# Key and value transfers of a whole batch (8 heads, 32 KB per partition), with the keys of a batch in two halves that have their own maxima

## The chip, the cores and the metric

The kernel runs on one core of a Trainium2 chip. The metric is the time of one execution in microseconds of the device. Three runs of the kernel before gave 190.66, 191.05 and 191.10 us; the median is 191.05.

The engines are named as in the profile: PE is the matmul engine (PEld its weight loads), DVE the vector engine, ACT the scalar engine, POOL GpSimd, and SP the engine that issues nearly all transfers here.

## The reference

One token of each of 8 batches passes through two branches, which a gate joins. All arrays are bfloat16. Branch A is attention over the last W = 1024 keys of a cache, with 16 query heads that share 8 key and value heads of 256 values each; branch B is a small MLP.

```python
g = sigmoid((x * gate_w).sum(-1, keepdims=True))           # x: (8, 1, 448)
q = (x @ wq).reshape(8, 1, 16, 256)                        # wq: (448, 4096)
k, v = k_cache[:, :, 3072:4096], v_cache[:, :, 3072:4096]  # (8, 8, 1024, 256), each head for 2 query heads
p = softmax(q k^T / 16)
a = (p v).reshape(8, 1, 4096) @ wo                         # wo: (4096, 448)
b = gelu(layernorm(x) @ w1 + b1) @ w2 + b2                 # hidden width 1792
out = g * a + (1 - g) * b
```

The window of keys and values is 8 batches x 8 heads x 1024 x 256 values, 33.55 MB of keys and as much of values, 67.1 MB of the 77.7 MB that the kernel reads.

## The kernel before

**Slots and loads.** Everything big goes through a ring of RING = 9 slots of 16 KB per partition (`ring`). `plan` is the list of loads in order; `pump` issues a load as soon as the program text has released enough slots with `done`, and the load itself then waits on SP until the slot's last readers are finished. SP issues in order, so a load that waits holds back the ones after it. The order is: keys of unit 0 in two parts, wq in two slots, w1, w2, then keys of unit u and values of unit u - 2 in turn, the last two values, and wo in two slots (the last piece cut in three, so that the end waits for little).

**Units.** A unit u (16 of them, NQ) is four key heads of one batch. `kv_loader` puts 4 heads x 1024 keys into a slot: partition p = 4 s + a holds 32 consecutive keys (NCK) of head a, segment s of 32. That is one row of 16 KB in memory for each partition, 2.1 MB in all.

**What a unit does.** `turn_keys` transposes half a slot in 32 x 32 blocks on DVE (line 357). `scores` puts the maskings of foreign heads (line 423) and eight matmuls (line 429) into half of a 1024-column PSUM tile S; two halves make a unit. `top` takes the maximum per partition (line 441), `share` joins the maxima of partitions by a matmul (449), `expo` makes the exponential with the row sums (455, 458). `turn` transposes the exponentials (471), `total` sums the row sums by a matmul (482), `invert` makes their reciprocals (492, 493), `values` multiplies with the values in 16 matmuls into PO (501) and takes the first half of it (510), `gather` adds the second half (516), and `finish` puts the normalized heads into oT (531, 534).

**The order of work.** It is written out by hand (`manual_schedule`): each engine carries its instructions out in the order of the program text. The loop at line 614 interleaves units: at u it turns and scores unit u, takes maxima and exponentials of unit u - 1, turns and multiplies unit u - 2 (LAG), and finishes unit u - 3. Before the loop come constants, `norm_and_gate`, the keys of unit 0, `query` (which makes qw, the query weights, from line 365 on), `mlp_hidden`, scores of unit 0 and `mlp_out` (line 592). After it come the rest of the last two units, `spread_rows` (656, 663), `project` (672), which multiplies with wo, and the final mix (690).

**Buffers that matter here.** Three transposed key tiles (`ktpool`), two S tiles, two small PSUM tiles shared by mz, den and fin (`ps_sm`), one PO, and one PSUM tile shared by hT, bb and A_ps (`ps_misc`).

Of the kernel before, what the change touches and what calls it, by code (L numbers as in the profile page):

```python
# [18 lines left out]
def kernel(  # L19
# [40 lines left out]
    RQ = QUAD * rep  # L60
    NQ = NB * Hkv // QUAD
    SK = P // QUAD
    NCK = W // SK
    NH = 2
    CH = NCK // NH
    NU = NQ
    SLOT = 8192
# [3 lines left out]
    WO_PARTS = [[(0, NJ8)]] * (NHQ - 1) + [[(0, 4), (4, 6), (6, 8)]]  # L71
    RING = 9
    LAG = 2
# [13 lines left out]
    ktpool = ctx.enter_context(tc.tile_pool(name="ktpool", bufs=3))  # L87
    epool = ctx.enter_context(tc.tile_pool(name="epool", bufs=2))
    opool = ctx.enter_context(tc.tile_pool(name="opool", bufs=LAG + 1))
# [19 lines left out]
    def kv_loader(src, u, parts):  # L109
        b, half = divmod(u, Hkv // QUAD)  # L110
        v = src[b, half * QUAD : (half + 1) * QUAD, kv_base:Sk, :].rearrange(
            "a (s c) d -> s a (c d)", c=NCK
        )

        def load(t):
            n = NCK * Dh // parts
            for i in range(parts):
                nc.sync.dma_start(  # L118
                    t[:, i * n : (i + 1) * n], v[:, :, i * n : (i + 1) * n]
                )  # L120

        return load
# [22 lines left out]
    def add_kv(name, src, u, parts=1):  # L145
        add((name, u), kv_loader(src, u, parts))
# [8 lines left out]
    add_kv("k", A_k_cache, 0, parts=2)  # L155
    add(("wq", 0), rows_loader([wq_m[:, 0 : 2 * HD]]))
    add(("wq", 1), rows_loader([wq_m[:, 2 * HD : 3 * HD], wq_t]))
    add(("w1",), rows_loader([w1_m, w1_t]))
    add(("w2",), rows_loader([w2_v]))
    for u in range(1, NQ):  # L160
        add_kv("k", A_k_cache, u)
        if u >= LAG:
            add_kv("v", A_v_cache, u - LAG)
    for u in range(NQ - LAG, NQ):
        add_kv("v", A_v_cache, u)
    for q in range(0, NHQ, 2):
        add(
            ("wo", q),
            rows_loader(
                [  # L170
                    wo_v[:, q + i, j0 * D : j1 * D]
                    for i in range(2)
                    for j0, j1 in WO_PARTS[q + i]
                ]
            ),
        )
# [4 lines left out]
    consts.tile([P, 448], BF16, name="pad")  # L181
# [37 lines left out]
    AREA = P + BLK  # L219
    qw = consts.tile([P, NJ, NU, AREA], BF16)  # L220
# [23 lines left out]
    for h in range(2):  # L244
# [18 lines left out]
    nc.vector.reduce_sum(sel2[:], pairs, axis=AXIS.X)  # L263
    nc.vector.reduce_sum(own[:], pairs.rearrange("p q i -> p i q"), axis=AXIS.X)
    head = consts.tile([BLK, QUAD], F32)
    nc.vector.reduce_sum(
        head[:],
        ident[0:BLK, 0:BLK].rearrange("p (s a) -> p a s", a=QUAD),
# [6 lines left out]
    for i in range(rep):  # L275
        nc.vector.tensor_copy(
            foreign[0:BLK, :].rearrange("p (b r) -> p b r", b=QUAD)[:, :, i:RQ:rep],
            head[:].rearrange("p (o a) -> p o a", o=1).to_broadcast([BLK, QUAD, QUAD]),
        )
# [73 lines left out]
    def turn_keys(u, hf):  # L353
        kn = slot("k", u)
        kt = ktpool.tile([P, CH, NK, BLK, NPAR], BF16, tag="kt", name="kt")
        KT[u, hf] = kt
        nc.vector.transpose(  # L357
            kt[:].rearrange("p c k x r -> p (c k x r)").bitcast(WORD),
            kn[:, hf * CH * Dh : (hf + 1) * CH * Dh].bitcast(WORD),
        )  # L360
        if hf == NH - 1:
            done()

    def query():
        for r in range(NR + 1):
            w, o = slot("wq", r // 2), (r % 2) * HD
            for n in range(W // QN):
                for t in range(QUAD):
                    col = t * W + n * QN
                    half, c = divmod(col, HH) if r == NR else (0, col)  # L370
                    nc.tensor.matmul(  # L371
                        Sq[32 * t : 32 * t + NB, n * QN : (n + 1) * QN],
                        lhsT=xT[:, r + half, :],
                        rhs=w[:, o + c : o + c + QN],
                        start=(r == 0),
                        stop=(r == NR),
                        skip_group_check=True,
                    )
        done(2)
# [15 lines left out]
        qp = ps_s.tile([P, NJ, NU, QUAD, RQ], F32, tag="S", name="qp")  # L395
        for j in range(NJ):
            for kk in range(NK // NJ):
                for par in range(NPAR):
                    nc.tensor.matmul(
                        qp[:, j, :, kk * NPAR + par, :],  # L400
                        lhsT=pick[:, kk, par, :],
                        rhs=qd[:, j].rearrange("p b h q i -> p (b h) (q i)"),
                        start=True,
                        stop=True,
                    )
        for b in range(QUAD):
            rows = slice(BLK * b, BLK * (b + 1))
            for j in range(NJ):
                dst = qw[rows, j, :, BLK * b : BLK * (b + 1)]
                src = qp[rows, j].rearrange("p u m q -> p u (m q)")  # L410
                if j == 0:
                    nc.scalar.copy(dst, src)  # L412
                else:
                    nc.vector.tensor_copy(dst, src)  # L414
# [3 lines left out]
    def scores(u, hf):  # L418
# [7 lines left out]
        for k in range(NK):  # L426
            for par in range(NPAR):
                j, m = k // (NK // NJ), k % (NK // NJ) * NPAR + par
                nc.tensor.matmul(  # L429
                    S[u][:, cols],  # L430
                    lhsT=qw[:, j, u, m * RQ : m * RQ + P],
# [19 lines left out]

    def expo(u):
        mz = soft.pop(u)
        nmx = epool.tile([P, 1], F32, tag="nmx", name="nmx")
        nc.vector.reduce_max(nmx[:], mz[:], axis=AXIS.X, negate=True)  # L455
        E = epool.tile([P, NCK // PAIR, BLK, PAIR], BF16, tag="E", name="E")
        rowsum = epool.tile([P, 1], F32, tag="rowsum", name="rowsum")
        nc.scalar.activation(  # L458
            E[:].rearrange("p c x i -> p c i x"),
            S.pop(u)[:].rearrange("p (c i x) -> p c i x", i=PAIR, x=BLK),  # L460
            ACT.Exp,
            bias=nmx[:],
            scale=1.0,
            accum_out=rowsum[:],
        )
        soft[u] = (E, rowsum)

    def turn(u):
        E, rowsum = soft.pop(u)
        ET = epool.tile([P, NCK // PAIR, BLK, PAIR], BF16, tag="ET", name="ET")  # L470
# [4 lines left out]
        soft[u] = (ET, rowsum)  # L475
# [3 lines left out]
    def total(u):  # L479
        ET, rowsum = soft.pop(u)  # L480
        den[u] = ps_sm.tile([P, 1], F32, tag="sm", name="den")
        nc.tensor.matmul(  # L482
            den[u][:], lhsT=rowden[:], rhs=rowsum[:], start=True, stop=True
        )
        soft[u] = ET

    rsel = {}

    def invert(u):
        rsel[u] = opool.tile([P, RQ], F32, tag="rsel", name="rsel")  # L490
        rb = epool.tile([P, 1], F32, tag="rb", name="rb")
        nc.vector.reciprocal(rb[:], den.pop(u)[:])  # L492
        nc.scalar.activation(rsel[u][:], sel2[:], ACT.Copy, scale=rb[:])  # L493

    def values(u):
        ET = soft.pop(u)
        vn = slot("v", u)
        NG = NCK // PAIR
        for c in range(NG):
            t = c % QUAD  # L500
            nc.tensor.matmul(  # L501
                PO[32 * t : 32 * t + PAIR * RQ],
                lhsT=ET[:, c, 0:RQ, :],
                rhs=vn[:, PAIR * c * Dh : PAIR * (c + 1) * Dh],
# [3 lines left out]
        done()  # L508
# [17 lines left out]
    def finish(u):  # L526
        b, half = divmod(u, Hkv // QUAD)
        os_, rs = soft.pop(u), rsel.pop(u)
        sm = ps_sm.tile([P, NJ, RQ], F32, tag="sm", name="fin")
        for j in range(NJ):  # L530
            nc.tensor.matmul(  # L531
                sm[:, j, :], lhsT=os_[:, j::NJ], rhs=rs[:], start=True, stop=True
            )
        nc.scalar.copy(  # L534
            oT[:, half * RQ : (half + 1) * RQ, :, b].rearrange("p h j -> p j h"), sm[:]
        )
# [70 lines left out]
    for hf in range(NH):  # L607
        turn_keys(0, hf)
    query()
    hs = mlp_hidden()  # L610
    for hf in range(NH):
        scores(0, hf)
    mlp_out(hs)
    for u in range(1, NQ):
        turn_keys(u, 0)
        scores(u, 0)
        if u >= LAG + 1:
            gather(u - LAG - 1)
        if u >= LAG:
            turn(u - LAG)  # L620
            total(u - LAG)
        if u >= LAG + 1:
            finish(u - LAG - 1)
        top(u - 1)
        share(u - 1)
        turn_keys(u, 1)
        if u >= LAG:
            values(u - LAG)
            invert(u - LAG)
        scores(u, 1)  # L630
        expo(u - 1)
    u = NQ - 1
    A_ps = ps_misc.tile([P, DO], F32, tag="misc", name="A_ps")
    gather(u - 2)
    finish(u - 2)
    turn(u - 1)
    total(u - 1)
    values(u - 1)
    top(u)
    share(u)  # L640
    invert(u - 1)
    expo(u)
    gather(u - 1)
    finish(u - 1)
    turn(u)
    total(u)
    invert(u)
# [19 lines left out]
    def project(q):  # L667
        w = slot("wo", q - q % 2)
        for j in range(NJ8):
            o = ((q % 2) * NJ8 + j) * D  # L670
# [9 lines left out]
    HALF = NHQ // 2  # L680
    spread_rows(0, HALF)
    values(u)
    gather(u)
    finish(u)
    project(0)
    spread_rows(HALF, NHQ)
    for q in range(1, NHQ):
# [43 lines left out]
```

## Time and profile before

| | |
|---|---|
| median of three runs | 191.05 us |
| the profiled execution | 191.06 us |
| its span, first to last instruction | 189.3 us |
| DVE busy, share of the span | 128.1 us, 68% |
| PE busy | 134.2 us, 71% |
| ACT busy | 43.1 us, 23% |
| bytes moved | 77.84 MB, 411 GB/s over the span |
| mean granted PE clock | 0.869 |
| line 357, transposition of half a slot of keys | 32 x 2306 ns |
| line 441, maximum over 1024 columns | 16 x 1187 ns |
| line 458, exponential of 1024 columns | 16 x 1387 ns |
| line 471, transposition of exponentials | 16 x 697 ns |
| line 510, first half of PO | 16 x 473 ns |
| issue to landing, values of a unit | 36.5 us |
| issue to landing, keys of a unit | 38.8 us |

In the page, a row of digits stands for 40 equal slices of the span: a digit is the busy share in tenths. The chain is followed back from the last instruction to what released each step. In the table by stretches, each row gives the start and end in us from the span's start, the length, busy time and instruction count of the engines, the granted clock, the busy share of the transfer engines and the rate. In the timeline, a row gives start and duration in us, the engine, the line, what is written and read, and in brackets the idle time before it and what ended that.

### The profile page before, as it was taken

The numbers are of one execution on the slowest core, as the hardware profiler recorded it, in microseconds if no ns is written. First come the engines' busy times: TensorE is split into PE (matmuls) and PEld (weight loads), VectorE is DVE, ScalarE is ACT, GpSimd is POOL, SyncE is SP. The second block draws the span as 40 slices with busy tenths as digits, with TensorE's granted clock in tenths as the row PEclk, the third lists the DMA queues.
The fourth block names the chain that finished last, engine by engine and source line by source line (L and its number), as shares of the span: only waits on it lengthen the run. The fifth ranks groups of instructions, "written<-read, shape, count | busy, mean of one in ns | idle before, by whom it ended". The sixth has DMA issues, their size and how long they took to land.

```text
span 189.3 us, 2502 instructions
## 1 busy us (share of the span) xinstructions
PE 134.2 (71%) x1013; PEld 69.8 (37%) x1022; DVE 128.1 (68%) x186; ACT 43.1 (23%) x91; POOL 5.0 (3%) x7
## 2 busy tenths in 40 slices
PE   0036899894878588866669985977499839399772
PEld 0021784441434143424225431533153414153461
DVE  7866266995949494949494949494958686772610
ACT  2031220313040404040401340314004404004510
POOL 8100000000000000000000000000000000000000
PEclk9999999999699966999955897999858999756955
DMA  5999999999999999999999999999999999999980
GB/s 188 422 424 434 428 435 431 422 422 440 429 433 429 426 436 426 429 436 433 429 426 433 428 436 422 433 433 426 436 426 433 436 426 426 436 433 426 410 356 14
DMA packets 6733, 77.84 MB, mean 411 GB/s; under 512 B 945, under 2 KB 1346, under 8 KB 1986
## 3 DMA queue, kind: packets, MB, share of 16 engines
q1 hardware_dynamic: 6512, 77.67, 96.5%
q8 instruction: 7, 0.11, 0.2%
q10 hardware_dynamic: 210, 0.02, 0.1%
q14 instruction: 4, 0.03, 0.0%
HBM read 77.68 MB, written 0.01 MB: 410 GB/s over the span
## 4 chain that ended last, share of the span: by engine, by line
DMA 84%; PE 8%; DVE 3%; ACT 1%; SPq 1%; issue 1%; ACTq 0%
DMA slot<-in_A_k_cache_dram 77%; DMA slot<-in_A_wq_dram 7%; PE S L429 3%; PE A_ps L672 2%; PE PO L501 2%; DVE kt L357 1%; PE fin L531 1%; ACT E L458 1%; SPq L118 1%; DVE mx L441 1%; ACT first L510 1%; DVE ET L471 0%; SPq L134 0%; PE mz L449 0%; DVE os__1552 L516 0%
## 5 line engine op out<-in xcount | busy, mean ns | idle before, releaser
L357 DVE STREAM_TRANSPOSE kt<-slot 128x2048 int32<-128x2048 int32 x32 | 73.7, 2306 | 33.7 <-DMA slot<-in_A_k_cache_dram 33.7
L429 PE MATMUL S<-kt,qw 128*128 128x512 bf16 x256 | 72.9, 433 | 30.5 <-DVE kt L357 26.7
L429 PEld LDWEIGHTS <-qw 128*128 128x128 bf16 x256 | 27.0, 106 | 69.4 <-issue 49.4
L458 ACT ACTIVATE E<-S,nmx 128x1024 bf16<-128x1024 f32 x16 | 22.2, 1387 | 2.6 <-DVE nmx L455 2.6
L534 ACT CAST oT<-fin 128x16 bf16<-128x16 f32 x16 | 3.6, 226 | 79.8 <-PE fin L531 79.8
L501 PE MATMUL PO<-slot,ET 128*16 128x512 bf16 x256 | 20.0, 441 | 0.1
L441 DVE TENSOR_REDUCE mx<-S 128x1 f32<-128x1024 f32 x16 | 19.0, 1187 | 0.3 <-PE S L429 0.3
L510 ACT ACTIVATE first<-PO,own 128x256 f32<-128x256 f32 x16 | 7.6, 473 | 29.2 <-PE PO L501 28.2
L471 DVE STREAM_TRANSPOSE ET<-E 128x512 int32<-128x512 int32 x16 | 11.2, 697 | 2.2 <-ACT E L458 2.2
L449 PE MATMUL mz<-m,same 128*128 128x4 f32 x32 | 6.8, 284 | 4.2 <-ACT oT L534 4.1
L423 PE MATMUL S<-place,foreign 128*128 128x512 bf16 x23 | 9.4, 409 | 0.1
L482 PEld LDWEIGHTS den<-rowsum,rowden 128*128 128x128 f32 x32 | 7.3, 234 | 3.9 <-issue 1.7
L449 PEld LDWEIGHTS mz<-m,same 128*128 128x128 f32 x32 | 5.7, 219 | 6.1 <-ACT oT L534 5.3
L501 PEld LDWEIGHTS <-ET 128*16 128x16 bf16 x256 | 5.3, 94 | 5.5 <-issue 2.3
L423 PEld LDWEIGHTS <-foreign 128*128 128x128 bf16 x32 | 3.2, 99 | 9.7 <-issue 7.9
L482 PE MATMUL den<-rowsum,rowden 128*128 128x1 f32 x32 | 5.2, 232 | 0.4 <-ACT E L458 0.4
L414 DVE CAST qw<-qp 32x512 bf16<-32x512 f32 x4 | 2.7, 687 | 3.4 <-ACT qw L412 3.4
L371 PE MATMUL Sq<-slot,xT 128*8 128x512 bf16 x32 | 3.9, 616 | 1.5 <-DMA slot<-in_A_wq_dram 1.5
L493 ACT ACTIVATE rsel<-sel,rb 128x8 f32<-128x8 f32 x16 | 4.7, 295 | 1.1 <-DVE rb L492 1.1
L455 DVE TENSOR_REDUCE nmx<-mz 128x1 f32<-128x4 f32 x16 | 2.3, 146 | 3.5 <-PE mz L449 3.5
L292 POOL MEMSET qw<- 128x5120 bf16 x1 | 4.4, 4364 | 0.0
L443 DVE TENSOR_SCALAR m<-block,mx 128x4 f32<-128x4 f32 x16 | 3.7, 229 | 0.6
(135 smaller groups left out, 84.9 us busy)
## 6 DMA issues: line engine op xcount, KB each, us to landing
slot<-in_A_v_cache_dram SPq DMA_DIRECT2D x16, 2048.0 KB, 36.5
slot<-in_A_k_cache_dram SPq DMA_DIRECT2D x15, 2048.0 KB, 38.8
slot<-in_A_wo_dram SPq DMA_DIRECT2D x3, 896.0 KB, 30.7
slot<-in_A_k_cache_dram SPq DMA_DIRECT2D x2, 1024.0 KB, 7.1
slot<-in_A_wq_dram SPq DMA_DIRECT2D x1, 2048.0 KB, 11.5
slot<-in_B_w_dram SPq DMA_DIRECT2D x1, 1568.0 KB
slot<-in_B_w_dram SPq DMA_DIRECT2D x1, 1344.0 KB
slot<-in_A_wq_dram SPq DMA_DIRECT2D x1, 1024.0 KB, 13.2
```

The source lines that it names most:

```text
L292: nc.gpsimd.memset(qw[:], 0.0)
L357: nc.vector.transpose(kt[:].rearrange("p c k x r -> p (c k x r)").bitcast(WORD), kn[:, hf * CH * Dh : (hf + 1) * CH * Dh].bitcast(WORD),)
L423: nc.tensor.matmul(S[u][:, cols], lhsT=foreign[:], rhs=place[:], start=True, stop=False)
L429: nc.tensor.matmul(S[u][:, cols], lhsT=qw[:, j, u, m * RQ : m * RQ + P], rhs=kt[:, :, k, :, par], start=False, stop=(k == NK - 1 and par = ...
L441: nc.vector.reduce_max(mx[:], S[u][:], axis=AXIS.X)
L449: nc.tensor.matmul(mz[:], lhsT=same[:], rhs=m4[:], start=True, stop=True)
L458: nc.scalar.activation(E[:].rearrange("p c x i -> p c i x"), S.pop(u)[:].rearrange("p (c i x) -> p c i x", i=PAIR, x=BLK), ACT.Exp, bias=n ...
L471: nc.vector.transpose(ET[:].rearrange("p c r i -> p (c r i)").bitcast(WORD), E[:].rearrange("p c x i -> p (c x i)").bitcast(WORD),)
L482: nc.tensor.matmul(den[u][:], lhsT=rowden[:], rhs=rowsum[:], start=True, stop=True)
L493: nc.scalar.activation(rsel[u][:], sel2[:], ACT.Copy, scale=rb[:])
L501: nc.tensor.matmul(PO[32 * t : 32 * t + PAIR * RQ], lhsT=ET[:, c, 0:RQ, :], rhs=vn[:, PAIR * c * Dh : PAIR * (c + 1) * Dh], start=(c < QUA ...
L510: nc.scalar.activation(first[:], PO[:, 0, :], ACT.Copy, scale=own[:, 0:1])
```

## The change

A slot holds all 8 heads of a batch: 32 KB per partition, 4.2 MB, with partition p = 8 s + a and 64 consecutive keys each. The ring has 4 slots in place of 9. wq has one slot in place of two, wo one in place of two (with the same six pieces), keys 0 and values 7 come in two parts, and w2 is loaded after all keys and values.

A unit is now half of the keys of a batch (512 keys) for all 8 heads; there are still 16 units, with two halves of scores each, and the matmuls and transpositions of a unit keep their number and their shape (the ET columns used in `values` are 32 in place of 16). Both units of a batch have their own maxima and exponentials. `expo` of the second unit takes the smaller of the two negated maxima (`low`) and makes two weights from it (`part`), `total` multiplies the two row sums with them and sums over the partitions, `invert` makes two scaled selections, and `finish` joins both units by them. So `total`, `invert` and `finish` run once a batch; `finish` has four matmuls in place of two.

In the loop, DVE transposes the keys from unit 2 on (the four halves of batch 0 before the query). Values lag by three units in place of two, and `mlp_out` moves from before the loop to after the last `finish`. `project` waits for all heads, where the kernel before projected its first quarter earlier.

```diff
-    RQ = QUAD * rep
-    NQ = NB * Hkv // QUAD
-    SK = P // QUAD
-    NCK = W // SK
+    RQ = Hkv * rep
+    SEG = P // Hkv
+    NCK = W // SEG
     NH = 2
-    CH = NCK // NH
-    NU = NQ
-    SLOT = 8192
+    NU = NB * NH
+    NCU = NCK // NH
+    CH = NCU // 2
+    SLOT = NCK * Dh
...
-    RING = 9
-    LAG = 2
+    RING = 4
+    LAG = 3
...
-    ktpool = ctx.enter_context(tc.tile_pool(name="ktpool", bufs=3))
+    ktpool = ctx.enter_context(tc.tile_pool(name="ktpool", bufs=4))
...
-    def kv_loader(src, u, parts):
-        b, half = divmod(u, Hkv // QUAD)
-        v = src[b, half * QUAD : (half + 1) * QUAD, kv_base:Sk, :].rearrange(
-            "a (s c) d -> s a (c d)", c=NCK
-        )
+    def kv_loader(src, b, parts):
+        v = src[b, :, kv_base:Sk, :].rearrange("a (s c) d -> s a (c d)", c=NCK)
...
-    add_kv("k", A_k_cache, 0, parts=2)
-    add(("wq", 0), rows_loader([wq_m[:, 0 : 2 * HD]]))
-    add(("wq", 1), rows_loader([wq_m[:, 2 * HD : 3 * HD], wq_t]))
+    add_kv("k", A_k_cache, 0, parts=NH)
+    add(("wq",), rows_loader([wq_m, wq_t]))
     add(("w1",), rows_loader([w1_m, w1_t]))
+    for b in range(1, NB):
+        add_kv("k", A_k_cache, b)
+        add_kv("v", A_v_cache, b - 1)
+    add_kv("v", A_v_cache, NB - 1, parts=NH)
     add(("w2",), rows_loader([w2_v]))
...
     def turn_keys(u, hf):
-        kn = slot("k", u)
+        b, h = divmod(u, NH)
+        kn = slot("k", b)
...
-        if hf == NH - 1:
+        if h == NH - 1 and hf == 1:
             done()
...
     def expo(u):
+        b, h = divmod(u, NH)
         mz = soft.pop(u)
...
+        nc.vector.reduce_max(nmx[:, h : h + 1], mz[:], axis=AXIS.X, negate=True)
+        if h == NH - 1:
+            low = epool.tile([P, 1], F32, tag="low", name="low")
+            nc.vector.tensor_reduce(low[:], nmx[:], op=ALU.min, axis=AXIS.X)
...
+        if h == NH - 1:
+            nc.scalar.activation(
+                part[:, 1 : 1 + NH], nmx[:], ACT.Exp, bias=low[:], scale=-1.0
+            )
...
+    def total(b):
+        _, rowsum, part = stat.pop(b)
+        both = epool.tile([P, NH], F32, tag="both", name="both")
+        nc.vector.scalar_tensor_tensor(
+            both[:], in0=rowsum[:], scalar=1.0, in1=part[:, 1 : 1 + NH],
+            op0=ALU.mult, op1=ALU.mult, accum_out=part[:, 0:1],
+        )
+        den[b] = ps_sm.tile([P, 1 + NH], F32, tag="sm", name="den")
+        nc.tensor.matmul(den[b][:], lhsT=rowden[:], rhs=part[:], start=True, stop=True)
...
+    def invert(b):
...
+        nc.vector.reciprocal(rb[:], d[:, 0:1])
+        for h in range(NH):
+            nc.vector.tensor_scalar(
+                rsel[b][:, h, :], sel2[:], scalar1=rb[:],
+                scalar2=d[:, 1 + h : 2 + h], op0=ALU.mult, op1=ALU.mult,
+            )
...
+    def finish(b):
+        rs = rsel.pop(b)
+        os_ = [soft.pop(b * NH + h) for h in range(NH)]
         sm = ps_sm.tile([P, NJ, RQ], F32, tag="sm", name="fin")
         for j in range(NJ):
+            for h in range(NH):
+                nc.tensor.matmul(
+                    sm[:, j, :], lhsT=os_[h][:, j::NJ], rhs=rs[:, h, :],
+                    start=(h == 0), stop=(h == NH - 1),
+                )
+        nc.scalar.copy(oT[:, :, :, b].rearrange("p h j -> p j h"), sm[:])
...
-    mlp_out(hs)
-    for u in range(1, NQ):
-        turn_keys(u, 0)
+    for u in range(1, NU):
+        v, g = u - LAG, u - LAG - 1
+        last = u >= 2 and (u - 2) % NH == NH - 1
+        if u >= NH:
+            turn_keys(u, 0)
         scores(u, 0)
+        if g >= 0:
+            gather(g)
+        if u >= 2:
+            turn(u - 2)
+        if last:
+            total((u - 2) // NH)
+        if g >= 0 and g % NH == NH - 1:
+            finish(g // NH)
         top(u - 1)
         share(u - 1)
+        if u >= NH:
+            turn_keys(u, 1)
+        if v >= 0:
+            values(v)
+        if last:
+            invert((u - 2) // NH)
         scores(u, 1)
         expo(u - 1)
+    u = NU - 1
+    gather(u - 3)
     turn(u - 1)
+    values(u - 2)
     top(u)
     share(u)
+    gather(u - 2)
+    finish(NB - 2)
     expo(u)
+    values(u - 1)
+    turn(u)
+    total(NB - 1)
     gather(u - 1)
+    invert(NB - 1)
+    values(u)
+    gather(u)
+    finish(NB - 1)
+    mlp_out(hs)
+    A_ps = ps_misc.tile([P, DO], F32, tag="misc", name="A_ps")
...
-    HALF = NHQ // 2
-    spread_rows(0, HALF)
-    values(u)
-    gather(u)
-    finish(u)
-    project(0)
-    spread_rows(HALF, NHQ)
-    for q in range(1, NHQ):
+    spread_rows(0, NHQ)
+    for q in range(NHQ):
         project(q)
```

## The prediction

> **What bounds the kernel now.** I read the page first (engines, slices, chain), then the busy table by stretches, then the timeline of the last 30 us.
>
> ```profile
> span 189.3 us, 2502 instructions
> ...
> PE 134.2 (71%) x1013; PEld 69.8 (37%) x1022; DVE 128.1 (68%) x186; ACT 43.1 (23%) x91; POOL 5.0 (3%) x7
> ...
> PEclk9999999999699966999955897999858999756955
> DMA  5999999999999999999999999999999999999980
> ...
> DMA 84%; PE 8%; DVE 3%; ACT 1%; SPq 1%; issue 1%; ACTq 0%
> ```
>
> No engine is full, but the DMA row is nines from the second slice to the last but one, and 84% of the chain is transfers. So everything that lies beside the transfers is free until it delays one. By stretches (columns: length, busy time and count of PE, PEld, DVE, ACT, POOL, then clock, DMA share, GB/s):
>
> ```profile
> 45.30:162.06 116.76, 86.53 (x498) 42.00 (x504) 83.97 (x96) 26.81 (x60) 0.00 (x0) 0.87 1.01 430
> ...
> 177.00:181.00 4.00, 2.30 (x38) 1.39 (x38) 1.56 (x6) 2.40 (x6) 0.00 (x0) 0.94 1.02 428
> ...
> 184.50:185.00 0.50, 0.50 (x32) 0.38 (x24) 0.00 (x0) 0.00 (x0) 0.00 (x0) 0.50 0.33 117
> 185.00:186.00 1.00, 0.87 (x40) 0.61 (x28) 0.07 (x1) 0.00 (x0) 0.00 (x0) 0.50 0.00 0
> ```
>
> Keys and values (rows of 16 KB) run at 430 GB/s, the last weights (rows of 7 KB) at 428; the last byte lands at about 185.0. The timeline shows what follows the last keys:
>
> ```profile
> 152.34 2.31 DVE L357 STREAM_TRANSPOSE kt<-slot 128x2048 int32<-128x2048 int32 x1 [2.70 <-DMA slot<-in_A_k_cache_dram]
> 154.70 1.90 PE L429 MATMUL S<-kt,qw 128*128 128x512 bf16 x8 [3.00 <-DVE kt L357]
> ...
> 161.01 0.38 PE L423 MATMUL S<-place,foreign 128*128 128x512 bf16 x1
> 162.08 2.31 DVE L357 STREAM_TRANSPOSE kt<-slot 128x2048 int32<-128x2048 int32 x1 [2.75 <-DMA slot<-in_A_k_cache_dram]
> ...
> 164.45 3.57 PE L429 MATMUL S<-kt,qw 128*128 128x512 bf16 x8 [3.06 <-DVE kt L357]
> ...
> 183.41 2.46 PE L672 MATMUL A_ps<-slot,oP 128*8 128x112 bf16 x96
> ...
> 185.93 0.33 DVE L690 SCALAR_TENSOR_TENSOR res<-A_ps,gg_s,mixb 128x112 bf16<-128x112 f32 x1 [1.93 <-PE A_ps L672]
> ```
>
> The last keys land at 162.06 and the last projection matmul ends at 185.87, 0.9 us after the last byte: two tails, of compute and of transfer, end almost together. That is where this change can win or lose. The two S rows also show the clock: eight matmuls take 1.90 us after one idle stretch of 3.0 us and 3.57 us after another.
>
> The sum is made against the profiled execution: 191.06 us, 189.3 of it span. The median is 191.05, so nothing is shifted.
>
> **Bytes and rows.** The bytes are the same. Rows of keys and values grow from 16 to 32 KB. A row's fixed cost, from 428 GB/s at 7 KB and 430 at 16 KB (per engine 268 and 610 ns): 2.2 ns; rounding of the two rates allows 0 to 4.5. Each of 16 engines saves about 120 rows: 0 to 0.55 us. I take 0.3, the middle. If a 32 KB row is cut in two on the way, it is 0. So the last byte lands at 184.7, and no tail can end before 185.0 (a hop and the last piece's 8 matmuls at 26 ns): a gain of at most 0.9 us, or 1.2 with all of the 0.55.
>
> One rule speaks against eight heads in one transfer, whose starts lie 2 MB apart. The Trainium skill, "DMA: Bandwidth & Descriptors", section "Latency and other measured facts", gives 164 GB/s where rows have a 2 MiB pitch and about 214 where they do not; by it the 67 MB (156 us at 430) would grow by about 47 us. The trace already has four heads at that pitch at 430, next to contiguous weights at 428, so I put this at nothing.
>
> **Slots.** SP's issues fall from 45 to 29, of 0.53 us each, all well ahead of their transfers (36 to 39 us to landing now). A 4.19 MB transfer takes 9.75 us. The slot of keys b is wanted again three transfers (29 us) after it landed and is free after the fourth transposition, at about 14.3 us, 16 at half clock (below). The slot of values is free about 11 us before it is wanted. At the start 2.1 MB more of keys stand ahead of wq (4.9 us) and 24 of the query's 32 matmuls wait for one landing (about 1.4), so qw is ready some 6 us later (33 for 27.2), mlp_hidden moves with it, and unit 2 starts at about 41 instead of at its keys' landing at 35. Keys 3 want their slot at 63; it is free at about 57. So the transfers stay packed, with 6 us to spare; past that each microsecond would count in full.
>
> **What moves.** In the loop DVE's wait for keys comes once in two units: 4.6 us instead of 2.7 twice. Behind it on DVE stand gather, turn and top of earlier units, and PE and ACT wait for those; PE's gap grows from 3.0 to about 4.4 us. Added per batch: low (0.15 us, as nmx), the weights' exponential (0.20, as gth), a product (0.2) and two scalings (0.16 each) for two rsel (0.295 each) and one reciprocal and den removed. All this lies beside transfers.
>
> w2 moves on SP behind all keys and values, and mlp_out from between units 0 and 1 to after the last finish. Behind the last keys there are now v6, v7, w2 and wo, 13.67 MB, where there were three values and wo, 9.96 MB. At 430 GB/s that is 8.6 us: the last keys land at 162.06 - 8.6 - 0.3 = 153.2. But two units follow them, not one.
>
> **The tail, from the landing of the last keys as 0, at full clock.** Unit 14 has neither den nor fin and goes like the unit at 152.34: its second half of scores ends at 8.85 (8.83 there). DVE starts unit 15 at 7.1; scores to 11.35; gather 0.44, turn 0.70, top 1.19 + 0.23 and the next transposition end at 14.25; PE meanwhile den 0.3, fin (eight instructions now, 2 x 0.61), copy and hop 0.35, mz 0.38, values 1.04, foreign 0.39, then scores from 15.05 to 16.95. Exp of unit 14 ends at 16.8, its turn at 17.45, top(15) at 18.9, mz 19.3, finish(6) 20.5. Its copy stands ahead of the last exp on ACT, which so runs from 20.75 to 22.35, and with the weights' exponential to 22.6. Then first(14) 23.1, gather 23.65, values(15) 24.75, first and gather 25.8, finish(7) 27.0, mlp_out (60 matmuls at 15 to 18 ns) 28.1, mixb 28.5, which frees the buffer for A_ps, its memset and the wider oP copy 29.2, and 128 matmuls: 2.0 at 15.4 ns (as bb) or 3.3 at 25.7 (as A_ps). End 31.2 at full clock. v6, v7 and w2 land at 9.8, 19.5 and 23.3, ahead of their use.
>
> Half clock: from 180.6 on the trace's tail ran at 0.50 in a stretch with gaps like these, so I take it here: fin 2.0 (+0.8), mlp_out +0.5, projection +1.3 and a hop: 33.9. The unit after the long gap: if only its first eight matmuls are slow, as at 47.63, the later slack swallows most, +0.6; two or three slow stretches, as after 164.45, +2.0 to +2.75. Unknown from below: 0, if the gap falls well.
>
> The skill has a rule for it ("TensorE: Matmul & The Clock Gate", section "HAM oscillation — how this bites in real kernels"): idle gaps over about 3.4 us put the clock to half. The rows above show half clock after 3.06 us and full after 3.00; the rule would make every 4.4 us gap a slow start, which means the +0.6 at least, without it the sum would be 0.6 less.
>
> Sum: 153.2 + 33.9 + 0.6 = 187.7 against 185.87: +1.8 us, 192.9.
>
> **Rivals.**
> A, the forecast: the compute tail ends last, at half clock in part. +1.2 (full clock in units 14 and 15) to +4.3 (three slow stretches, no gain in rows): 192.3 to 195.4. For it: clock 0.50 at the end now, the longer gap, mlp_out in the tail. Against: the waits in the tail are my sums. Chance 0.62.
> B, faster: the full clock holds, the compute tail takes 31.2 and ends at 184.4, under the transfers; then the last byte decides, 185.0: 190.2, at best 189.9. It decides if the tail stays under 31.8. For it: clock 1.00 from 174 to 180; against: 0.50 after. Chance 0.18.
> C, in between: the tail takes 32.1 to 33.2, half clock only in the last matmuls: within 0.6 us, 191.1. Chance 0.14.
> D, starvation: PE at half clock takes more than 19.5 us for a pair (10.4 a unit, as the one at 164.45), slots come free late and the DMA row gets holes: 1.3 us in each of some five pairs, 6 less slack and the tail: 196 to 199. Against: two thirds of the units run at full clock. Chance 0.06.
>
> **How the numbers follow.** 0.3% (0.57 us) is about what a measurement can tell from no change. Faster is B, 0.18; same C, 0.14; slower A and D, 0.68. The time is A's with one slow stretch, 192.9. For 8 in 10, the range takes A but its end, C and most of B: 190.1 to 195.0; A alone has 192.0 to 195.4.
>
> **What would show it.** Right: DMA row without holes, last keys at about 153, about half as many DVE waits for keys but each near 4.6 us, last exp at about +21, last matmul at 186.5 to 189 with the last byte before 185. Wrong: holes in the DMA row (D), a rate above 433 or below 425 GB/s (rows), PE waiting for wo at the end (B), or clock 1.00 through the tail.

## The result: 351.43 us, and the profile after

The changed kernel takes 351.43 us (349.02 to 352.73) against 190.91 for the kernel before on the same chip: 1.8395 times as long, interval 1.8279 to 1.8512. The forecast was 192.9, in a range from 190.1 to 195.0. It missed by 158.5 us, and none of its rivals came near.

The page of the kernel after: span, engines, clock and DMA rows of the 40 slices, two groups, and two transfers.

```profile
span 348.3 us, 2419 instructions
...
PE 141.7 (41%) x982; PEld 70.1 (20%) x990; DVE 132.6 (38%) x218; ACT 39.9 (11%) x75; POOL 4.6 (1%) x7
...
PEclk9999996968558655766559675766559565787655
DMA  8999999999999999999999999999999999999994
GB/s 184 213 312 440 188 229 196 226 196 224 199 222 196 226 196 226 196 224 203 218 199 222 203 221 203 218 226 196 215 207 233 195 226 215 211 205 231 223 404 172
...
L347 DVE STREAM_TRANSPOSE kt<-slot 128x2048 int32<-128x2048 int32 x32 | 73.6, 2303 | 162.4 <-DMA slot<-in_A_k_cache_dram 162.3
...
L524 PE MATMUL PO<-slot,ET 128*32 128x512 bf16 x256 | 25.4, 538 | 56.3 <-DMA slot<-in_A_v_cache_dram 56.3
...
slot<-in_A_k_cache_dram SPq DMA_DIRECT2D x7, 4096.0 KB, 65.7
slot<-in_A_v_cache_dram SPq DMA_DIRECT2D x7, 4096.0 KB, 52.2
```

The engines work about as long as before (DVE 132.6 us for 128.1, PE 141.7 for 134.2), so the 159 us of longer span are not work. The DMA row is still nines without a hole, which the forecast had named as the sign that all is well. It is not: here the busy share is full although the rate has halved, so the share says that packets are under way and not how fast they move. The row under it tells the truth: about 210 GB/s in nearly every slice (184 to 235) in place of some 430, and over 400 again only in the two slices in which weights are loaded, one behind the first keys and one near the end. The keys and values alone are slow.

One stretch of the middle of the kernel (length; PE, PEld, DVE, ACT and POOL busy; clock; DMA share; GB/s):

```profile
60.00:310.00 250.00, 100.00 (x516) 45.52 (x520) 97.07 (x136) 26.20 (x51) 0.00 (x0) 0.68 1.00 211
```

Keys and values are 67.1 MB: 156 us at the 430 GB/s of the kernel before, 318 at 211. The difference, 162 us, is the whole loss of 160.5 (351.43 less 190.91).

The list of waits says the same from the engines' side (total us, times, longest; the first line is the kernel before), and the timeline shows one batch:

```profile
DVE kt L357 <- DMA slot<-in_A_k_cache_dram: 33.7, 14, 3.0
...
DVE kt L347 <- DMA slot<-in_A_k_cache_dram: 162.3, 8, 26.0
PE PO L524 <- DMA slot<-in_A_v_cache_dram: 56.3, 9, 8.5
```

```profile
215.40 2.31 DVE L347 STREAM_TRANSPOSE kt<-slot 128x2048 int32<-128x2048 int32 x1 [25.05 <-DMA slot<-in_A_k_cache_dram]
...
254.82 2.31 DVE L347 STREAM_TRANSPOSE kt<-slot 128x2048 int32<-128x2048 int32 x1 [24.78 <-DMA slot<-in_A_k_cache_dram]
```

From the keys of one batch to those of the next pass 39.4 us, in which 8.39 MB arrive: 213 GB/s. DVE waits for keys in 25 of them. The granted clock of PE, 0.68 in the stretch above, goes with these pauses; where a run below has the rate back, its stretch shows 0.87, as the kernel before does.

So the question for the experiments is not where the time is but why this transfer runs at half rate. Against the one before, the transfer has eight heads and not four, rows of 32 KB and not 16, 16 segments of keys in its outermost dimension and not 32, and its segments lie elsewhere. It also fills larger slots, in another order of work.

### The profile page after: what moved, and what is told of

Read it like the earlier page. It is cut to its first block, busy times and chain, and to the rows that moved or that the text cites. A ratio compares the mean times of both kernels' runs of the same rounds, so it can differ in the third digit from the quotient of the medians.

```text
span 348.3 us, 2419 instructions
## 1 busy us (share of the span) xinstructions
PE 141.7 (41%) x982; PEld 70.1 (20%) x990; DVE 132.6 (38%) x218; ACT 39.9 (11%) x75; POOL 4.6 (1%) x7
## 4 chain that ended last, share of the span: by engine, by line
another core or an unknown queue 47%; DVE 27%; DMA 22%; PE 2%; SPq 1%; issue 0%; ACT 0%
DVE kt L347 17%; DMA slot<-in_A_k_cache_dram 16%; DMA slot<-in_A_wo_dram 6%; DVE mx L431 4%; DVE ET L476 2%; PE S L419 1%; DVE rsel L507 1%; DVE m L433 1%; SPq L131 1%; PE PO L524 1%; ACT E L459 0%; DVE low L457 0%; DVE nmx L454 0%; DVE rb L505 0%
## 5 line engine op out<-in xcount | busy, mean ns | idle before, releaser
L419 PE MATMUL S<-kt,qw 128*128 128x512 bf16 x256 | 79.8, 465 | 111.1 <-DVE kt L347 108.4
L419 PEld LDWEIGHTS <-qw 128*128 128x128 bf16 x256 | 28.7, 112 | 153.2 <-issue 136.0
L524 PE MATMUL PO<-slot,ET 128*32 128x512 bf16 x256 | 25.4, 538 | 56.3 <-DMA slot<-in_A_v_cache_dram 56.3
L524 PEld LDWEIGHTS <-ET 128*32 128x32 bf16 x256 | 7.6, 118 | 63.9 <-issue 53.6
L439 PEld LDWEIGHTS mz<-m,same 128*128 128x128 f32 x32 | 6.8, 233 | 6.8 <-ACT oT L563 2.9
L563 ACT CAST oT<-fin 128x32 bf16<-128x32 f32 x8 | 2.4, 295 | 22.9 <-PE fin L556 22.9
L708 PE MATMUL A_ps<-slot,oP 128*8 128x112 bf16 x128 | 3.8, 292 | 2.5 <-DMA slot<-in_A_wo_dram 1.8
L361 PEld LDWEIGHTS <-xT 128*8 128x8 bf16 x32 | 1.1, 118 | 18.9 <-issue 18.9
L507 DVE TENSOR_SCALAR rsel<-sel,rb,den 128x16 f32<-128x16 f32 x16 | 4.0, 296 | 0.3
L280 POOL MEMSET qw<- 128x4608 bf16 x1 | 3.9, 3937 | 0.0
```

The source lines that it names most:

```text
L361: nc.tensor.matmul(Sq[32 * t : 32 * t + NB, n * QN : (n + 1) * QN], lhsT=xT[:, r + half, :], rhs=w[:, o + c : o + c + QN], start=(r == 0), ...
L419: nc.tensor.matmul(S[u][:, cols], lhsT=qw[:, j, u // NH * 2 + m, par * RQ : par * RQ + P], rhs=kt[:, :, k, :, par], start=False, stop=(k = ...
L439: nc.tensor.matmul(mz[:], lhsT=same[:], rhs=m4[:], start=True, stop=True)
L507: nc.vector.tensor_scalar(rsel[b][:, h, :], sel2[:], scalar1=rb[:], scalar2=d[:, 1 + h : 2 + h], op0=ALU.mult, op1=ALU.mult,)
L524: nc.tensor.matmul(PO[32 * t : 32 * t + PAIR * RQ], lhsT=ET[:, c, 0:RQ, :], rhs=vn[:, o : o + PAIR * Dh], start=(c < QUAD), stop=(c >= NG ...
```

## The experiments

The theories, which the expectations shorten to letters: E, that the number of segments decides, through the partitions that each transfer engine writes; against it, that the rows are too long (L), that the places read at the same time lie badly in memory (P), and that eight heads at once are too many (H). E was later sharpened to Q, which says how the engines get in each other's way.

**Transfers alone, seven patterns.** The kernel only loads, 16.8 MB a pattern, 128 partitions, and nothing is computed. Patterns in the order in which they run:

```
 K[i, 4h:4h+4, 3072:4096]   "a (s c) d -> s a (c d)", c=32   4 heads, 32 segments, rows of 16 KB (as before)
 K[i, :, 3072:4096]         ...                       c=64   8 heads, 16 segments, rows of 32 KB (as after)
 K[i, :, half of the keys]  ...                       c=32   8 heads, 16 segments, rows of 16 KB
 K[i, 0:4, 2048:4096]       ...                       c=64   4 heads, 32 segments, rows of 32 KB
 flat "(a s c) d -> s a (c d)", a=8, c=64                    8 blocks 512 KB apart, 16 segments, rows of 32 KB
 the same, c=32                                              8 blocks 256 KB apart, 16 segments, rows of 16 KB
 flat "(p c) d -> p (c d)", p=128                            128 rows of 32 KB on end
```

> Only transfers: seven stages of 16.8 MB from the key cache into four 32 KB buffers, each stage waiting for the one before; all computation is left out. Stage 1: four heads, rows of 16 KB (before). 2: eight heads, rows of 32 KB (after). 3: eight heads, rows of 16 KB next to each other. 4: four heads, 32 segments, rows of 32 KB. 5: eight blocks 512 KB apart, 16 segments, rows of 32 KB. 6: eight blocks 256 KB apart, 16 segments, rows of 16 KB. 7: 128 contiguous rows of 32 KB. Theory E (an outermost dimension of 16 segments, eight partitions each, is what halves the rate): 1, 4 and 7 at about 430 GB/s, 2, 3, 5 and 6 at about 210. Theory P (segments 32 KB apart): 1, 3, 6 at 430, 2, 4, 5 at 210. Theory H (eight starts 2 MB apart instead of four): 2 and 3 at 210, the others at 430. Theory L (a row of 32 KB is slow by itself): 2, 4, 5 and 7 at 210.

The stretches, one for each pattern (DVE and POOL busy, clock, DMA share, GB/s):

```profile
5.00:37.00 32.00, 0.00 (x0) 0.00 (x0) 1.00 1.01 432
50.00:120.00 70.00, 0.33 (x2) 0.00 (x0) 1.00 1.01 210
135.00:200.00 65.00, 0.16 (x1) 0.00 (x0) 1.00 1.01 214
210.00:240.00 30.00, 0.32 (x2) 0.00 (x0) 1.00 1.00 433
255.00:320.00 65.00, 0.32 (x2) 0.00 (x0) 1.00 0.99 210
335.00:400.00 65.00, 0.00 (x0) 0.00 (x0) 1.00 1.00 218
408.00:438.00 30.00, 0.32 (x2) 0.00 (x0) 1.00 1.01 437
```

The half rate is there without any of the kernel's work. Rows of 32 KB run at 433 and 437 GB/s, rows of 16 KB at 214 and 218: length is not it. Eight blocks 256 or 512 KB apart are as slow as eight heads 2 MB apart: distance is not it. All patterns with 16 segments are slow, all with 32 or 128 are fast. But every slow pattern here also reads eight blocks at once, so these seven do not yet part the number of segments from the number of blocks; two later runs, on partitions and on engines, do.

**In the changed kernel: rows of 16 KB, still 16 segments.** Each slot is filled by two transfers, one for each half of the keys.

```diff
-        v = src[b, :, kv_base:Sk, :].rearrange("a (s c) d -> s a (c d)", c=NCK)
+            for i in range(NH):
+                lo = kv_base + i * (W // NH)
+                v = src[b, :, lo : lo + W // NH, :].rearrange(
+                    "a (s c) d -> s a (c d)", c=NCU
+                )
+                nc.sync.dma_start(t[:, i * n : (i + 1) * n], v)
```

> The changed kernel, with each slot loaded in two transfers: the first half from 512 keys that lie together, the second from the other 512, so that the 16 segments of a head are 16 KB long and 16 KB apart as before; eight heads and an outermost dimension of 16 stay. Theory P and L: the rate goes back to 430 GB/s and the time to 190 to 195 us. Theory E and H: 340 to 355 us, as changed.

It took 340.81 us, 1.7831 times the kernel before (1.7699 to 1.7963):

```profile
60.00:150.00 90.00, 41.54 (x201) 18.96 (x203) 33.72 (x50) 9.97 (x19) 0.00 (x0) 0.67 1.01 213
```

The rows have the size of those before and the rate is still about half (227 GB/s from 150 to 300 us; why this kernel is 10.6 us shorter than the changed one is not shown). Row length, and with it the pitch of neighbouring rows, falls in the kernel too.

**In the kernel before: eight heads and 16 segments, and nothing else.** Slots of 16 KB, ring, units and maxima stay as they were; only the source of a load changes.

```diff
-        v = src[b, half * QUAD : (half + 1) * QUAD, kv_base:Sk, :].rearrange(
-            "a (s c) d -> s a (c d)", c=NCK
-        )
+        lo = kv_base + half * (W // 2)
+        v = src[b, :, lo : lo + W // 2, :].rearrange("a (s c) d -> s a (c d)", c=NCK)
```

> The kernel before with one edit: each 2.1 MB transfer reads 512 keys of eight heads (16 segments, rows of 16 KB) where it read 1024 keys of four heads (32 segments, rows of 16 KB). Slots, bytes, row length, order and all instructions stay; the maskings then belong to other heads, so the output is not the reference's. Theory E (outermost dimension of 16): keys and values at 211 GB/s instead of 430, 156 us of transfers become 318, so 345 to 355 us. Rival (it is the 32 KB slot and its order that starve the transfers): 190 to 192.

343.56 us, 1.7976 times (1.794 to 1.8012), a little under the range that theory E gave:

```profile
60.00:150.00 90.00, 45.74 (x192) 19.59 (x192) 29.57 (x33) 10.84 (x24) 0.00 (x0) 0.65 1.01 213
```

One expression in one function makes 152 of the 160 us. The slots, the two halves and their weights are not needed for it.

**The changed kernel with 128 segments.** All is left as it is but the source: the same number of bytes, from two whole heads on end, so that keys and values stand in other places than the computation wants.

```diff
-        v = src[b, :, kv_base:Sk, :].rearrange("a (s c) d -> s a (c d)", c=NCK)
+        v = src[b, 0:2].rearrange("h k d -> (h k) d").rearrange("(p c) d -> p (c d)", p=P)
```

> The changed kernel with one edit: a slot is loaded from 4.2 MB that lie together, 128 rows of 32 KB, so it holds other keys and values and the output is not the reference's; bytes, slots, rings, units and all instructions stay. Theory E: 430 GB/s again, and the time is then what the prediction summed for the rest of the change: 192.9 us, 190.1 to 195.0 with its bounds, last keys at about 153, the compute tail at half clock in part. Rival (four slots of 32 KB cannot keep the transfers packed at full rate either): holes in the transfers and 196 us or more.

190.92 us (190.54 to 191.45) against 191.23, a ratio of 0.9989 (0.9978 to 0.9999). With the rate given back, the rest of the change costs nothing that can be measured.

```profile
45.00:152.00 107.00, 78.25 (x457) 36.57 (x462) 82.64 (x116) 24.38 (x46) 0.00 (x0) 0.87 1.01 433
```

This is the kernel in which the other steps of the prediction can be read; the next section does so.

**Which partitions.** What is left is how a transfer of 16 segments is laid over engines and partitions. These kernels load 64 partitions at a time, and compute nothing; the first partition is moved.

```
 v = K[i, 4*h : 4*h+4, 3072:4096, :].rearrange("a (s c) d -> s a (c d)", c=64)   # 16 segments of 4 heads
 eng.dma_start(bufs[i][p0 : p0 + 64, :], v)      # p0 = 0, 32, 64; then 0 and 64 in turn
```

> Only transfers; all computation is left out. Each transfer has 16 segments of four heads, rows of 32 KB, 2.1 MB, into 64 partitions, four for each engine; only the first partition differs. Stage 1 (four of them): partitions 0 to 63. 2: 32 to 95. 3: 64 to 127. 4 (eight of them): 0 to 63 and 64 to 127 in turn on one queue. 5: the same, after 1 MB for the first eight segments alone, which gives half of the engines a head start of one transfer. 6: low halves on SP's queue and high ones on ACT's. Theory Q (engines whose partitions lie 32 apart in one half of the 128 write through the same door and halve each other, so that what counts is which partitions are written at one time): 1, 3 and 4 at about 215 GB/s, 2 at 430, 5 nearer to 430 than 4 if the head start lasts, 6 between. Theory R (16 segments as outermost dimension are slow to read, wherever they go): 1, 2, 3, 4 and 6 all at about 215. The Trainium skill, page SBUF — State Buffer, section Door 1: The DMA port swizzle, gives such a map of partitions to 16 ports, in which 32 further is the same port and 64 further is another.

Stretches for p0 = 0, for p0 = 32, for p0 = 64, for 0 and 64 in turn on one queue, and for 0 on one queue beside 64 on another:

```profile
15.00:45.00 30.00, 0.00 (x0) 0.00 (x0) 1.00 0.97 199
53.00:69.00 16.00, 0.16 (x1) 0.00 (x0) 1.00 0.99 426
78.00:108.00 30.00, 0.16 (x1) 0.00 (x0) 1.00 1.00 209
120.00:187.00 67.00, 0.00 (x0) 0.00 (x0) 1.00 1.01 215
...
275.00:350.00 75.00, 0.16 (x1) 0.00 (x0) 1.00 1.02 224
```

The same bytes from the same addresses into 64 partitions run at 199 GB/s from partition 0 on and at 426 from partition 32 on. The source can't be the cause, then; the partitions written are. Four heads are enough for the half rate, so it is not the number eight either. The rates fit if partitions 0 to 63 share something, 64 to 127 share its twin, and 32 to 95 reach both. To write low and high halves in turn hardly helps (215), nor do two queues (224).

In the part with a head start for half of the engines, the 1 MB meant to go just ahead of it was issued at the very start of the kernel (0.73 us), so that part only repeated the two halves in turn (209 GB/s from 191 to 270 us). It was run again with the order written out:

> Only transfers, as in the run before that shifted the partitions, with the order now as written. Stage 1: 16 segments of four heads into partitions 0 to 63, four transfers. 2: into 32 to 95. 3: 0 to 63 and 64 to 127 in turn, eight transfers. 4: the same after 1 MB for the first eight segments alone, which holds half of the engines back by the time of one transfer's rows. Theory Q (two engines behind one door at the same time): 1 and 3 at 215 GB/s, 2 at 430, and 4 at 430 as long as the head start lasts, for then one engine of each pair writes low and the other high partitions. Rival (only the number of partitions or segments counts): 4 at 215 like 3.

p0 = 0, p0 = 32, in turn, and then in turn after 1 MB that only the first eight segments' engines load (its first 10 us, and the rest):

```profile
8.00:40.00 32.00, 0.00 (x0) 0.00 (x0) 1.00 0.97 197
49.00:64.00 15.00, 0.00 (x0) 0.00 (x0) 1.00 1.04 448
78.00:145.00 67.00, 0.00 (x0) 0.00 (x0) 1.00 1.02 211
155.00:165.00 10.00, 0.00 (x0) 0.00 (x0) 1.00 0.99 223
165.00:215.00 50.00, 0.00 (x0) 0.00 (x0) 1.00 1.01 287
```

287 lies between the theories. The packets of 32 KB in the trace say a little more: most take 1.21 us in the fast stage and 2.57 in the slow one, and in this last stretch anything from 1.2 to 2.6. So some rows get the full rate, some the half, and most lie between. That agrees with Q, if engines held apart in time collide in part; why the head start is not kept is not shown.

**How many engines, and which.** Eight heads and n segments go into 8n partitions from p0 on; nothing is computed.

```
 v = K[i, :, 3072 : 3072 + 64*n, :].rearrange("a (s c) d -> s a (c d)", c=64)
 nc.sync.dma_start(bufs[i][p0 : p0 + 8*n, :], v)      # (n, p0) = (4, 0), (8, 0), (8, 32), (16, 0)
```

> Only transfers, in the changed kernel's shape with fewer segments: n segments of eight heads, rows of 32 KB, eight neighbouring partitions for each of n engines, four transfers a stage. Stage 1: n = 4, partitions 0 to 31. 2: n = 8, partitions 0 to 63. 3: n = 8, partitions 32 to 95. 4: n = 16, partitions 0 to 127. A full-rate engine moves 430 / 16 = 27 GB/s. Theory Q (engines whose partitions are 32 apart in one half share doors, and nothing else is wrong with the shape): 1 at 4 x 27 = 108, 2 no more than that although twice the engines work, 3 at 8 x 27 = 215, 4 at 210. Rival (an engine with eight neighbouring partitions runs at half rate whoever else works): 54, 107, 107 and 210.

```profile
8.00:38.00 30.00, 0.00 (x0) 0.00 (x0) 1.00 0.25 109
50.00:120.00 70.00, 0.00 (x0) 0.00 (x0) 1.00 0.51 108
131.00:160.00 29.00, 0.00 (x0) 0.00 (x0) 1.00 0.50 216
176.00:245.00 69.00, 0.00 (x0) 0.00 (x0) 1.00 0.99 205
```

The DMA share fits one engine for each segment: 0.25 with four segments is four of 16 at work, 0.51 with eight is eight. An engine then writes eight neighbouring partitions, its eight heads. Four engines on partitions 0 to 31 move 109 GB/s, 27 each, which is what each of 16 has at 432. Eight engines on 0 to 63 move no more than four: 13.5 each. Eight engines on 32 to 95 have 27 each again, with eight heads and eight partitions to an engine as in the slow stages, so neither of the two is the cause. An engine loses half when another writes 32 partitions away in the same half of the 128, and with 16 segments every engine has such a partner. What stays open is how 32 segments are divided: the runs show their rate, not which engine writes which partition.

**Large slots alone.** The kernel before with slots of 32 KB (a ring of 4 in place of 9), each filled by two of its own transfers of four heads; units, maxima and the order of the computation as before.

```diff
-SLOT 8192, RING 9
+SLOT 16384, RING 4
+            for h in range(2):            # two units into the two halves of a slot
+                v = src[w, h * QUAD : (h + 1) * QUAD, kv_base:Sk, :].rearrange("a (s c) d -> s a (c d)", c=NCK)
...
+    for w in range(1, NB):
+        add_kv("k", A_k_cache, w)
+        add_kv("v", A_v_cache, w - 1)
```

> The kernel before with 32 KB slots alone: a slot holds two units side by side, in two transfers of the shape before (32 segments of four heads); wq, the MLP weights and wo have a slot each, four slots in all; units, maxima and order of work stay as before. Theory E: rate 430 GB/s, 190 to 193 us, the tail like before. Rival (big slots by themselves starve the transfers): 196 us or more, with holes in the row of transfers.

Keys and values come in turn, 4.19 MB of each, and the small weights share slots, as the ring is shorter. It took 192.54 us, 1.0074 times (1.0059 to 1.0089): inside the range of theory E, with a small loss. PE now waits for values:

```profile
PE PO L496 <- DMA slot<-in_A_v_cache_dram: 24.5, 6, 4.3
```

```profile
120.00:140.00 20.00, 14.46 (x83) 6.72 (x84) 14.58 (x17) 4.46 (x10) 0.00 (x0) 0.83 1.00 424
```

The order of the kernel before uses values two units after their keys, which is short when values come 4 MB at a time; from 20 to 160 us the transfers run at 424 to 431 GB/s for 428 to 434. That slots come free later is the likely reason, but no run tests it. The whole loss is 1.3 us, and not 160.

**The change with the transfer mended.** A slot of eight heads is filled by two transfers of four heads with 32 segments each. A half of a slot then holds four heads with all keys, not all heads with half of the keys, so the maskings and the offsets follow; all else of the change stays.

```diff
-        v = src[b, :, kv_base:Sk, :].rearrange("a (s c) d -> s a (c d)", c=NCK)
+            for f in range(2):
+                v = src[b, f * QUAD : (f + 1) * QUAD, kv_base:Sk, :].rearrange(
+                    "a (s c) d -> s a (c d)", c=NCU
+                )
...
+        lhsT=foreign[hf][:]                            # one masking for each half of a slot
+        o = (hf * NH + h) * CH * Dh                    # turn_keys
+        f, k = divmod(c, NG // 2)                      # values
+        o = ((f * NH + h) * (NG // 2) + k) * PAIR * Dh
```

> The changed kernel with all its computation, in which a slot is filled by two transfers of the shape before (32 segments of four heads, rows of 16 KB): half a slot holds four heads, and the maskings belong to the half instead of to the partition. Theory E: 430 GB/s, last keys at about 153.5, 190.7 to 191.8 us, no difference from the kernel before that a measurement would call a gain; rival (32 KB rows gave part of what the full-rate run reached): 192 or more.

191.11 us, a ratio of 1.0 (0.9989 to 1.0011), at 431 GB/s:

```profile
45.00:152.00 107.00, 78.62 (x465) 35.69 (x464) 85.80 (x119) 24.40 (x46) 0.00 (x0) 0.91 1.01 431
```

All 160 us are back.

**The same, with mlp_out earlier.** In the kernel above w2 is loaded before the last values, and mlp_out moves from behind the last finish to behind values of unit 14.

```diff
+    add(("w2",), rows_loader([w2_v]))
     add_kv("v", A_v_cache, NB - 1, parts=NH)
-    add(("w2",), rows_loader([w2_v]))
...
     values(u - 1)
+    mlp_out(hs)
...
     finish(NB - 1)
-    mlp_out(hs)
```

> The run above with two more moves: w2 is loaded ahead of the last values, and mlp_out stands behind the values of unit 14, where PE idles, instead of behind the last finish. In the full-rate run mlp_out, its mix and the wait for the shared buffer stood for about 1.9 us between the last finish and the spreading. If the compute tail ends last: 1.0 to 1.9 us less than the run above, 189.2 to 190.5. If the last transfer is what ends last (about 185.0 in the kernel before): not below 190.2, and at least 0.3 less than the run above.

191.06 us, 1.0003 (0.9992 to 1.0014): the gain is missing, of which both cases had expected at least 0.3 us. The last rows of the projection say why:

```profile
183.80 0.92 PE L717 MATMUL A_ps<-slot,oP 128*8 128x112 bf16 x32 [0.84 <-DMA slot<-in_A_wo_dram]
...
186.03 0.36 PE L717 MATMUL A_ps<-slot,oP 128*8 128x112 bf16 x8 [0.21 <-DMA slot<-in_A_wo_dram]
```

PE is early and waits for the last pieces of wo: the last byte sets the end. In the run above it already did: there PE waits for wo four times, the last time before the matmuls at 185.81. Work taken out of the compute tail no longer shows. Why the last piece comes there some 0.8 us later than the 185.0 of the kernel before is not shown. Over long stretches every fast pattern into 128 partitions lies between 424 and 437 GB/s, and the kernel before is at 430 already; none of these versions beats it by more than can be told.

## Why the prediction was wrong

**The step that failed** is in "Bytes and rows": "the last byte lands at 184.7", and behind it, under "Slots", "A 4.19 MB transfer takes 9.75 us". Both carry the 430 GB/s of the kernel before over to a transfer of another shape. Measured: 211 GB/s, 19.9 us for a transfer. I asked of the new transfer what its bytes, the length of its rows and the distance of its heads do to the rate, and the runs confirm all three as harmless. I did not ask how its outermost dimension, halved from 32 to 16, is divided over engines and partitions, and none of the rivals A to D did. The evidence that I leaned on, four heads 2 MB apart at 430, holds for four heads in 32 segments: the division had changed with the number of heads, since 128 partitions are segments times heads. What the runs showed in its place: with 16 segments each engine writes eight neighbouring partitions, another engine writes those 32 further on, and both run at half rate (eight engines move 108 GB/s on partitions 0 to 63 and 216 on 32 to 95). The one line of the prediction that fits is among its signs of failure, a rate below 425.

Rival D, starvation, would have been the nearest, as it ends with slow transfers; but its cause was slots that come free late, and the DMA row has no holes. Its own bound was 199.

The page "SBUF — State Buffer" of the Trainium skill, section "Door 1: The DMA port swizzle (why `[64,N]` ≈ `[32,N]`)", has the rule that bears on this: four neighbouring partitions write through one of 16 ports, those 32 further on through the same one and those 64 further on through another. The runs agree at each point that they touch: 109 for partitions 0 to 31, 108 for 0 to 63 and 216 for 32 to 95, with eight partitions to an engine. The map alone does not give the loss, though: by it 128 partitions reach all 16 ports, and the changed transfer has 205 to 210 there. That two engines must also write to one port at the same time is inferred from the rates; no view shows which port is written when. That four neighbouring partitions go together and not eight fits the run that moved the first partition: 16 segments of four heads give each engine four partitions, and on 32 to 95 all 16 engines together have 426 GB/s, so engines on neighbouring fours do not halve each other. Whether the grain is finer than four is not tested.

The other rule, weighed in the prediction, of a 2 MiB distance that costs bandwidth (the Trainium skill, "DMA: Bandwidth & Descriptors", section "Latency and other measured facts"), was rightly put at nothing for four heads: 432 and 433 GB/s. The page measured it on copies between tensors in HBM, which the prediction did not say. The slow transfers do not speak for it either, as blocks 256 KB apart are slow too.

**The other steps**, read in the changed kernel with 128 segments. They would have come to +1.8 us; measured is -0.3 in the medians, 190.92 for 191.23, within what can be told from no change, and +0.5 in the profiled executions' last matmuls (186.41 for 185.87), of which the one with 128 segments is the slowest of its ten runs (191.45). Its waits and its last 35 us:

```profile
DVE kt L349 <- DMA slot<-in_A_k_cache_dram: 24.2, 6, 5.3
```

```profile
153.08 2.31 DVE L349 STREAM_TRANSPOSE kt<-slot 128x2048 int32<-128x2048 int32 x1 [5.32 <-DMA slot<-in_A_k_cache_dram]
...
155.44 3.57 PE L421 MATMUL S<-kt,qw 128*128 128x512 bf16 x8 [5.52 <-DVE kt L349]
...
168.00 1.90 PE L421 MATMUL S<-kt,qw 128*128 128x512 bf16 x8 [0.16 <-DVE nmx L456]
...
173.34 1.41 ACT L461 ACTIVATE E<-S,nmx 128x1024 bf16<-128x1024 f32 x1
...
180.56 1.48 PE L621 MATMUL bb<-slot,hs 128*8 128x112 bf16 x56
...
183.25 3.16 PE L710 MATMUL A_ps<-slot,oP 128*8 128x112 bf16 x128 [0.66 <-DVE oP L701]
```

- Last keys at 153.2: held, 153.08. Waits for keys about half as many: held, 6 for 14. Near 4.6 us each: 4.0 on average, the longest 5.3.
- Eight slow matmuls after the long gap: held, 3.57 us after 5.5. That they cost 0.6: wrong. The second half of the last unit's scores ends 16.8 us after the landing (169.90), where the sum at full clock had 16.95. That row waits only 0.16 us, and for DVE: the 1.67 us that PE lost fell into slack on the way.
- Last exp at +20.75 and 0.6: 20.3. The last mlp_out at +29.4 and 0.6: it ends at 182.2, 29.1. Projection 3.3 us: 3.16. It ends at 186.41, 33.3 after the landing, where 34.5 was summed. It starts without waiting for wo, whose last bytes come soon after 184 (14 GB/s from 184 to 185, none after), so the compute tail ends last, as in A. The mechanism was right; the term that was mis-sized is the tail, 1.2 us too long, of which 0.6 are the slow start and 0.6 are spread over many waits. Without them, and with last keys 0.1 earlier, 0.5 is left of the +1.8 in the profiled execution, and nothing in the medians.
- Rows of 32 KB save 0.3 us: 433 GB/s for 430 would be about 1 us of the 156, and the last byte lands 0.9 earlier than the 185.0 of before. But rows of 16 KB reach 431 and 432 in other runs, so how much of it the rows give is not settled.
- Slots with 6 us to spare: held at full rate, with a DMA share of 0.96 or more in every stretch from 2 to 180 us; SP issues keys 3 at 54.8, where the slot was to be free at about 57. In the slow kernel it never mattered: a transfer of 19.9 us was issued 52 to 66 us before it landed.

Rival B's mechanism, the last byte as the end, is what the mended kernels show (PE waits for wo up to 186). It gives no change there and not the gain of 0.9 that B had, since the last byte did not come earlier.

## What to carry to other kernels

Before counting a transfer at the rate of another, ask how its outermost dimension is spread over the engines and which partitions each of them writes. An outermost dimension of 16 over 128 partitions gave 210 GB/s here, 32 or more gave 430, with the same bytes and rows of the same length. Read GB/s for each stage, never the DMA busy share alone, and when a whole layout is to be changed, first run the new transfer by itself: a kernel that only loads shows the half rate, and with it the 160 us.

## What the hardware showed that I had not expected

- A half rate with all 16 engines at a busy share of 1.00: 210 GB/s for 432, decided, for 64 partitions from one source, by the first partition alone (199 from partition 0 on, 426 from 32 on).
- Eight engines moving no more than four: 108 and 109 GB/s.
- Engines out of step do not make the loss go away: 1 MB of head start gave 287 GB/s, and two queues on the two halves 224.
